# Weight tiles of a retention and feed-forward kernel: first parts rounded by a casting transfer on GpSimd's queue instead of by ScalarE

## The chip, the cores and the metric

One core of one Trainium2 chip. The metric is the device time of one execution in microseconds (us). The engines are called as the profile calls them: PE (TensorE, with PEld for its weight loads), DVE (VectorE), ACT (ScalarE), POOL (GpSimd) and SP (SyncE, which issues most transfers here).

## The reference, cut to what matters

Retention over 8 batches, 8 heads, 576 positions and 64 channels gives x of 4608 tokens by 512. A feed-forward with a rational function between two matrix products follows:

```python
ret = scores * Dmat[None, :, :, :]          # scores = q k^T / 8, Dmat = gamma ** (i - j), causal
x = matmul(ret, v)                          # reshaped to 4608 x 512
h = x @ w_in                                # 512 -> 2048
P = a[0] + a[1] * h + a[2] * h2 + a[3] * h3
Q = 1.0 + np.abs(b[0]) * np.abs(h) + np.abs(b[1]) * h2
return (P / (Q + 1e-06)) @ w_out            # 2048 -> 512
```

The weights come as float64. Products are made with operands in two parts: a first part, rounded to the type that PE reads fast (fp32r), and a second part, the rest. Each product is three matmuls: first by first, first by second, second by first.

## The kernel before

The 4608 tokens are nine blocks b of 512. The 2048 inner columns are sixteen tiles f of 128. One step of the main loop (L728) is one pair (b, f). `gemm1` (L478) makes h(b, f) in PSUM with twelve matmuls. `ffn_p` to `ffn_q3` (L489 to L535) make the rational function on ACT and DVE. `ffn_hi` (L549, ACT) and `ffn_lo` (L555, DVE or POOL by the table LO) make g, the two parts of its result. `gemm2` (L568) adds g times the second weights into the accumulators, three or four steps later (`lag`, L645). Steps 0 to 7 are block 0 with tiles 0 to 7, steps 8 to 23 block 1 with all sixteen, steps 24 to 31 block 0 with tiles 8 to 15; the other blocks follow. `half` is 8. Retention is done in slices before the loop and as "visits" inside it.

Weights: 32 tiles, w0_f of w_in and w1_f of w_out. `load_weight` (L165) brings the float64 bits of one, `split_weight` (L170), a generator, makes its two parts. It goes on by one yield whenever `split_step` (L663) is called, so its pieces lie in one to three steps:

- ACT writes c from the high words and scales the low words in place (L188, L189).
- DVE joins them in c (L192): this is the weight in float32.
- ACT copies c, rounded, into the first part (L199).
- DVE or POOL, by the table WLO (L71), subtracts it from c and so makes the second part (L201).

c comes from the pool `cnv` (L108), which has four buffers: ACT may write a fifth c only when the subtraction that reads the first is done. Four of the tiles (w1_0 to w1_3, called late) lie in other buffers and are left as they are.

Names: the profile leaves out numbers, so "c", "w", "g" and "p" stand for all tiles of that kind. With numbers, w1_10 is tile 10 of w_out, c1_10 its float32 form, g1_9 the result of block 1, tile 9, h1_12 its input to the function.

The order of the work on each engine is that of the program (`InOrder`, L78), and the program's order in a step is one of the lists of names at L33 to L57, the same in both versions. POOL has one queue of instructions: one that waits holds all behind it. In the part of the program that matters here (steps 8 to 21), u lies in PSUM (`free_at`) in most steps.

Of the kernel before, what the change touches and what calls it, by code (L numbers as in the profile page):

```python
# [13 lines left out]
F32R = mybir.dt.float32r  # L14
# [3 lines left out]
AF = mybir.ActivationFunctionType  # L18
# [3 lines left out]
P = 128  # L22
B, H, S, D = 8, 8, 576, 64
NT = B * S
DM = H * D
# [45 lines left out]
WLO = "vector pool pool pool pool pool pool vector vector pool vector vector vector vector pool pool vector vector pool vector pool vector pool vector pool vector pool pool pool pool vector pool".split()  # L71
# [18 lines left out]
def retention_ffn(ctx: ExitStack, tc: tile.TileContext, qkv, w_in, w_out, consts, masks, out):  # L90
# [13 lines left out]
    wts = ctx.enter_context(tc.tile_pool(name="wts", bufs=1))  # L104
# [12 lines left out]
    pe, act, dve, pool = (InOrder(tc, e) for e in (nc.tensor, nc.scalar, nc.vector, nc.gpsimd))  # L117
# [43 lines left out]
    parts = {}  # L161
    plain, held = {}, []
    step = -1
# [6 lines left out]
    def split_weight(k):  # L170


        nm = f"{k[0]}_{k[1]}"
        words = bits[k].bitcast(I32).rearrange("p (c w) -> p c w", w=2)
        low, high = words[:, :, 0], words[:, :, 1]
        late = k[0] == 1 and str(k[1]) in PLAIN
        if late:
            i = PLAIN.index(str(k[1]))
            if i < 2:
                held.append(op.tile([P, 2, DM], F32, tag=f"o{1 - i}", name=f"held{i}"))  # L180
            cf = plain[k[1]] = held[i % 2][:, i // 2, :]
            c = cf.bitcast(I32)
        else:
            c = cnv.tile([P, DM], I32, tag="c", name=f"c{nm}")
            cf = c.bitcast(F32)


        act.activation(cf, high.bitcast(F32), AF.Prelu, scale=math.ldexp(1.0, -112), alpha=-math.ldexp(1.0, 32))  # L188
        act.activation(low, low.bitcast(U32), AF.Copy, scale=math.ldexp(7.49, -32))  # L189
        yield  # L190
        yield
        dve.scalar_tensor_tensor(c, c, 3, low, ALU.logical_shift_left, ALU.bitwise_or)  # L192
        yield
        yield
        while late and step < PLAIN_TO + PLAIN.index(str(k[1])):
            yield
        w = wts.tile([P, 2, DM], F32R, tag=f"w{nm}", name=f"w{nm}")
        del bits[k]
        act.activation(w[:, 0, :], cf, AF.Copy)  # L199
        engine = dve if WLO[len(parts)] == "vector" else pool  # L200
        engine.tensor_tensor(w[:, 1, :], cf, w[:, 0, :].bitcast(F32), ALU.subtract)  # L201
        parts[k] = w

# [435 lines left out]
    half = NF // 2  # L639
# [18 lines left out]
    def split_start(n):  # L658
        for k in [k for _, k in zip(range(n), splits)]:
            going.append([split_weight(k), 0])  # L660
            next(going[-1][0])
# [66 lines left out]
    for i in range(len(steps) + lag(len(steps))):  # L728
        step = i
# [69 lines left out]
```

## Time and profile before

| | |
|---|---|
| median of 3 runs | 870.05 us (868.37 to 870.51) |
| profiled execution, its own time | 871.07 us |
| its span, first to last instruction | 869.0 us |
| PE busy | 849.4 us (98%) |
| DVE busy | 773.4 us (89%) |
| ACT busy | 665.6 us (77%) |
| POOL busy | 130.8 us (15%), 107 instructions |

The span is what the trace shows; the 2.07 us between it and the execution's own time lie around it. A share of busy time is an average over the whole span, and the part of the program in which the weights of the later steps are split is only some 115 us of it, so the views below are cut to windows of that part.

### The profile page before, as it was taken

The numbers are of one execution on the slowest core, as the hardware profiler recorded it, in microseconds if no ns is written. First come the engines' busy times: TensorE is split into PE (matmuls) and PEld (weight loads), VectorE is DVE, ScalarE is ACT, GpSimd is POOL, SyncE is SP. The second block draws the span as 40 slices with busy tenths as digits, with TensorE's granted clock in tenths as the row PEclk, the third lists the DMA queues.
The fourth block names the chain that finished last, engine by engine and source line by source line (L and its number), as shares of the span: only waits on it lengthen the run. The fifth ranks groups of instructions, "written<-read, shape, count | busy, mean of one in ns | idle before, by whom it ended". The sixth has DMA issues, their size and how long they took to land.

```text
span 869.0 us, 18739 instructions
## 1 busy us (share of the span) xinstructions
PE 849.4 (98%) x7574; PEld 727.2 (84%) x7574; DVE 773.4 (89%) x1221; ACT 665.6 (77%) x1240; POOL 130.8 (15%) x107
## 2 busy tenths in 40 slices
PE   8899999999999999999999999999999999999997
PEld 6666787778888888888888888888888888888886
DVE  4998999999899889888889888888898988888995
ACT  3888999988767778777877787777877787767775
POOL 2523333631001110111111100011111111000000
PEclk9999999999999999999999999999999999999999
DMA  9896000032121112111211121101211121001001
GB/s 341 320 340 232 1 2 0 1 99 101 48 98 50 49 50 98 49 50 50 97 50 50 50 89 60 47 30 37 87 47 50 49 98 50 1 2 48 1 1 48
DMA packets 20774, 64.55 MB, mean 74 GB/s; under 512 B 2512, under 2 KB 2640, under 8 KB 20688
## 3 DMA queue, kind: packets, MB, share of 16 engines
q1 hardware_dynamic: 20528, 63.10, 20.6%
q8 instruction: 59, 0.97, 0.4%
q14 instruction: 27, 0.22, 0.1%
q10 hardware_dynamic: 160, 0.26, 0.1%
HBM read 53.91 MB, written 9.44 MB: 73 GB/s over the span
## 4 chain that ended last, share of the span: by engine, by line
PE 83%; DVE 10%; ACT 4%; issue 1%; DMA 1%; SPq 0%; POOL 0%; ACTq 0%; DVEq 0%; POOLq 0%
PE acc L86 39%; PE h L86 36%; DVE p L86 4%; PE ps L86 4%; DVE v L86 3%; PE y L86 2%; DVE c L86 1%; ACT free_at L86 1%; PE psNone L86 1%; DMA qk<-in_qkv 1%; ACT bits L86 1%; ACT g L86 1%; ACT c L86 0%; DVE qk L86 0%; ACT p L86 0%
## 5 line engine op out<-in xcount | busy, mean ns | idle before, releaser
L86 PE MATMUL h<-xhi,w 128*128 128x512 f32 x1152 | 367.8, 381 | 3.8 <-DVE p L86 1.9
L86 PE MATMUL acc<-w,g 128*128 128x512 f32 x1584 | 366.9, 381 | 3.0 <-ACT o L86 1.6
L86 PEld LDWEIGHTS acc<-w,g 128*128 128x128 f32 x1584 | 296.5, 189 | 47.6 <-ACT o L86 2.0
L86 PEld LDWEIGHTS h<-xhi,w 128*128 128x128 f32 x1152 | 217.7, 189 | 37.9 <-DVE p L86 3.1
L86 ACT ACTIVATE p<-h,const_sb 128x512 f32<-128x512 f32 x144 | 111.6, 775 | 165.0 <-PE h L86 158.4
L86 PE MATMUL h<-xlo,w 128*128 128x512 f32 x576 | 218.4, 379 | 0.1
L86 DVE TENSOR_TENSOR p<-p,h 128x512 f32<-128x512 f32 x144 | 98.6, 684 | 42.5 <-ACT u L86 40.1
L86 PEld LDWEIGHTS h<-xlo,w 128*128 128x128 f32 x576 | 108.9, 189 | 16.7 <-issue 1.1
L86 DVE SCALAR_TENSOR_TENSOR p<-p,const_sb,h 128x512 f32<-128x512 f32 x144 | 107.3, 745 | 4.0
L86 ACT ACTIVATE v<-u,absb 128x512 f32<-128x512 f32 x129 | 103.2, 800 | 0.4 <-DVE p L86 0.2
L86 DVE TENSOR_TENSOR v<-v,u 128x512 f32<-128x512 f32 x131 | 101.4, 774 | 0.2 <-ACT v L86 0.2
L86 DVE SCALAR_TENSOR_TENSOR p<-v,p 128x512 f32<-128x512 f32 x140 | 98.6, 704 | 3.3
L86 DVE SCALAR_TENSOR_TENSOR p<-p,const_sb,u 128x512 f32<-128x512 f32 x131 | 99.2, 758 | 1.2 <-ACT u L86 1.2
L86 POOL TENSOR_TENSOR S<-S,const_sb 128x256 f32<-128x256 f32 x32 | 27.2, 850 | 453.4 <-DVE S L86 453.4
L86 DVE SCALAR_TENSOR_TENSOR v<-v,u 128x512 f32<-128x512 f32 x131 | 89.4, 683 | 0.0
L86 ACT ACTIVATE u<-u 128x512 f32<-128x512 f32 x131 | 82.6, 630 | 4.3
L86 ACT ACTIVATE g<-p 128x512 fp32r<-128x512 f32 x132 | 82.8, 627 | 3.5 <-DVE p L86 3.0
L86 ACT ACTIVATE u<-v 128x512 f32<-128x512 f32 x131 | 81.9, 625 | 0.8 <-DVE v L86 0.8
L86 DVE TENSOR_TENSOR g<-p,g 128x512 fp32r<-128x512 f32 x115 | 78.6, 683 | 0.7 <-ACT g L86 0.7
L86 ACT ACTIVATE u<-h 128x512 f32<-128x512 f32 x131 | 76.7, 585 | 2.5 <-DVE v L86 2.4
L86 ACT ACTIVATE kv<-kv,const_sb 128x64 f32<-128x64 f32 x232 | 58.2, 333 | 4.5 <-DMA kv<-in_qkv 4.5
L86 POOL TENSOR_TENSOR qk<-qk,const_sb 128x512 f32<-128x512 f32 x31 | 48.6, 1566 | 38.8 <-DMA qk<-in_qkv 38.7
(93 smaller groups left out, 713.7 us busy)
## 6 DMA issues: line engine op xcount, KB each, us to landing
qk<-in_qkv SPq DMA_DIRECT2D x36, 512.0 KB, 4.1
kv<-in_qkv SPq DMA_DIRECT2D x32, 512.0 KB, 5.5
bits<-in_w_in SPq DMA_DIRECT2D x16, 512.0 KB, 8.1
bits<-in_w_out SPq DMA_DIRECT2D x16, 512.0 KB, 7.3
out<-o SPq DMA_DIRECT2D x28, 256.0 KB, 3.7
kv<-in_qkv SPq DMA_DIRECT2D x4, 256.0 KB, 7.0
out<-o SPq DMA_DIRECT2D x8, 128.0 KB, 2.1
out<-last SPq DMA_DIRECT2D x2, 256.0 KB, 2.4
```

Of the source, the lines that this page charges most:

```text
L86: return lambda *a, **k: self.tc.keep_in_program_order(method(*a, **k))
```

## The change

For a tile whose third piece falls in step 8 or later, and which is not late, the copy on ACT is taken out. A transfer from c into the first part, which casts to fp32r, is issued on POOL's queue one yield earlier, and the subtraction is always POOL's.

```diff
         dve.scalar_tensor_tensor(c, c, 3, low, ALU.logical_shift_left, ALU.bitwise_or)
         yield
+        moved = step >= half and not late
+        if moved:
+            w = wts.tile([P, 2, DM], F32R, tag=f"w{nm}", name=f"w{nm}")
+            pool.dma_start(w[:, 0, :], cf)
         yield
         while late and step < PLAIN_TO + PLAIN.index(str(k[1])):
             yield
-        w = wts.tile([P, 2, DM], F32R, tag=f"w{nm}", name=f"w{nm}")
+        if not moved:
+            w = wts.tile([P, 2, DM], F32R, tag=f"w{nm}", name=f"w{nm}")
+            act.activation(w[:, 0, :], cf, AF.Copy)
         del bits[k]
-        act.activation(w[:, 0, :], cf, AF.Copy)
-        engine = dve if WLO[len(parts)] == "vector" else pool
+        engine = dve if WLO[len(parts)] == "vector" and not moved else pool
         engine.tensor_tensor(w[:, 1, :], cf, w[:, 0, :].bitcast(F32), ALU.subtract)
```

It holds for 17 tiles: w0_8 to w0_15 and w1_7 to w1_15. ACT has 17 instructions fewer, DVE 7 fewer, POOL 17 transfers and 7 subtractions more. Three places of the order show it.

DVE, at the end of the step in which c0_10 is joined; w0_9 is the second part of a weight tile, p and v are the rational function's.

```order
 L86 TENSOR_TENSOR v1_4_1258<-v1_4_1258,free_at_1045 128x512
 L86 SCALAR_TENSOR_TENSOR p1_3_1203<-v1_3_1202,p1_3_1203 128x512
-L86 TENSOR_TENSOR w0_9_1288<-c0_9_1185,w0_9_1288 128x512
 L86 SCALAR_TENSOR_TENSOR c0_10_1241<-c0_10_1241,bits0_10_907 128x512
 L86 TENSOR_TENSOR p1_5_1309<-p1_5_1309,h1_5_1294 128x512
```

The subtraction is gone from DVE, and what stood behind it moves up by one place. It is the same for w0_8, w0_11, w0_12, w0_13, w0_14 and w1_14.

ACT, around the writing of c1_12, which takes the buffer of c1_10.

```order
 L86 ACTIVATE free_at_1045<-v1_10_1554 128x512
 L86 ACTIVATE free_at_1045<-free_at_1045 128x512
-L86 ACTIVATE w1_10_1631<-c1_10_1535 128x512
-L86 ACTIVATE w0_14_1634<-c0_14_1538 128x512
 L86 ACTIVATE c1_12_1637<-bits1_12_1181 128x512
 L86 ACTIVATE bits1_12_1181<-bits1_12_1181 128x512
```

Two copies are gone in front of c1_12.

POOL, from g1_9 to g1_11, before:

```order
L86 TENSOR_TENSOR g1_9_1608<-p1_9_1505,g1_9_1608 128x512
L86 TENSOR_TENSOR w1_10_1631<-c1_10_1535,w1_10_1631 128x512
L86 TENSOR_TENSOR g1_10_1660<-p1_10_1555,g1_10_1660 128x512
L86 TENSOR_TENSOR w1_11_1683<-c1_11_1582,w1_11_1683 128x512
L86 TENSOR_TENSOR w0_15_1686<-c0_15_1585,w0_15_1686 128x512
L86 TENSOR_TENSOR g1_11_1723<-p1_11_1604,g1_11_1723 128x512
```

and with the change:

```order
L86 TENSOR_TENSOR g1_9_1608<-p1_9_1505,g1_9_1608 128x512
L86 DMA w1_10_1627<-c1_10_1535 128x512
L86 DMA w0_14_1629<-c0_14_1538 128x512
L86 TENSOR_TENSOR w1_10_1627<-c1_10_1535,w1_10_1627 128x512
L86 TENSOR_TENSOR w0_14_1629<-c0_14_1538,w0_14_1629 128x512
L86 TENSOR_TENSOR g1_10_1660<-p1_10_1555,g1_10_1660 128x512
L86 DMA w1_11_1679<-c1_11_1582 128x512
L86 DMA w0_15_1681<-c0_15_1585 128x512
L86 TENSOR_TENSOR w1_11_1679<-c1_11_1582,w1_11_1679 128x512
L86 TENSOR_TENSOR w0_15_1681<-c0_15_1585,w0_15_1681 128x512
L86 DMA w1_12_1729<-c1_12_1637 128x512
L86 TENSOR_TENSOR g1_11_1723<-p1_11_1604,g1_11_1723 128x512
```

Each subtraction now stands behind the transfer that writes its operand, on the same queue, and g1_11 stands behind three transfers and two subtractions that follow g1_10, where before two subtractions stood.

## Rows read from the trace of the kernel before

**Rows 1.** Busy time in windows: window, then us (count) by engine, PEclk, DMA share, GB/s.

```profile
103.72:132.31 28.59, 28.59 (x132) 24.86 (x132) 27.76 (x43) 27.55 (x44) 6.82 (x5) 1.00 0.01 1
132.31:157.13 24.82, 21.68 (x97) 17.87 (x97) 24.60 (x39) 23.08 (x39) 8.11 (x6) 1.00 0.00 0
157.13:191.10 33.97, 32.74 (x410) 27.43 (x410) 33.80 (x47) 29.09 (x59) 19.17 (x14) 1.00 0.11 33
300.00:700.00 400.00, 400.00 (x3850) 348.90 (x3849) 357.65 (x574) 302.97 (x591) 41.79 (x32) 1.00 0.17 57
```

**Rows 2.** Waits of PE, 75 to 195 us: us in total, times, longest us.

```profile
PE h L86 <- DVE p L86: 1.9, 3, 0.7
PE acc L86 <- ACT o L86: 1.6, 1, 1.6
PE h L86 <- ACT w L86: 1.3, 1, 1.3
PE y L86 <- issue: 0.5, 1, 0.5
PE acc L86 <- DVE w L86: 0.4, 1, 0.4
PE acc L86 <- POOL g L86: 0.3, 1, 0.3
```

**Rows 3.** Groups of instructions, 75 to 195 us: the pieces that split the weights.

```profile
L86 POOL TENSOR_TENSOR w<-c,w 128x512 fp32r<-128x512 f32 x10 | 13.5, 1353 | 22.9 <-ACT w L86 22.9
L86 ACT ACTIVATE w<-c 128x512 fp32r<-128x512 f32 x18 | 10.8, 623 | 0.0
L86 DVE TENSOR_TENSOR w<-c,w 128x512 fp32r<-128x512 f32 x8 | 5.4, 680 | 0.0
```

**Rows 4.** Timeline of DVE: start us, us; the subtraction of w0_8 and the next.

```profile
106.19 0.68 DVE L86 TENSOR_TENSOR w<-c,w 128x512 fp32r<-128x512 f32 x1
106.80 0.82 DVE L86 SCALAR_TENSOR_TENSOR c<-c,bits 128x512 int32<-128x512 int32 x1
```

**Rows 5.** DMA issues of the page: count, KB each, median us to landing.

```profile
bits<-in_w_in SPq DMA_DIRECT2D x16, 512.0 KB, 8.1
out<-o SPq DMA_DIRECT2D x28, 256.0 KB, 3.7
...
out<-o SPq DMA_DIRECT2D x8, 128.0 KB, 2.1
out<-last SPq DMA_DIRECT2D x2, 256.0 KB, 2.4
```

**Rows 6.** Timeline of POOL: the subtractions of g1_1, g1_9, g1_10 and g1_11.

```profile
101.76 1.27 POOL L86 TENSOR_TENSOR g<-p,g 128x512 fp32r<-128x512 f32 x1 [2.27 <-ACT g L86]
...
149.12 1.28 POOL L86 TENSOR_TENSOR g<-p,g 128x512 fp32r<-128x512 f32 x1 [4.68 <-ACT g L86]
...
155.56 1.27 POOL L86 TENSOR_TENSOR g<-p,g 128x512 fp32r<-128x512 f32 x1 [3.52 <-issue]
...
161.48 1.29 POOL L86 TENSOR_TENSOR g<-p,g 128x512 fp32r<-128x512 f32 x1 [1.80 <-issue]
```

**Rows 7.** Timeline of ACT: first part of g1_9; copies of w1_10, w0_14; c1_12.

```profile
148.37 0.68 ACT L86 ACTIVATE g<-p 128x512 fp32r<-128x512 f32 x1
...
150.06 1.14 ACT L86 ACTIVATE w<-c 128x512 fp32r<-128x512 f32 x2
152.08 0.88 ACT L86 ACTIVATE c<-bits 128x512 f32<-128x512 f32 x1 [0.88 <-POOL w L86]
```

**Rows 8.** Timeline of PE: the products of g1_10 and g1_11, 24 matmuls.

```profile
159.80 5.45 PE L86 MATMUL acc<-w,g 128*128 128x512 f32 x24
```

**Rows 9.** Timelines of DVE and POOL near 183 us: one operation alone, and one beside POOL.

```profile
182.92 1.77 DVE L86 SCALAR_TENSOR_TENSOR p<-p,const_sb,u 128x512 f32<-128x512 f32 x1
...
188.57 0.75 DVE L86 SCALAR_TENSOR_TENSOR p<-p,const_sb,u 128x512 f32<-128x512 f32 x1
...
182.67 1.48 POOL L86 TENSOR_TENSOR w<-c,w 128x512 fp32r<-128x512 f32 x1 [6.66 <-ACT w L86]
```

## The prediction

> **What bounds the kernel now.** I read the windows first, because the page's shares are averages over stages that differ. From 300 to 700 us PE is busy all the time and DVE and ACT have room (357.65 and 302.97 of 400) [rows 1]: what is gained or lost ahead of that stretch is carried to the end one to one, since nothing behind can catch up on PE. The change lies in 103 to 191 us. There DVE is busy 27.76 of 28.59, then 24.60 of 24.82, then 33.80 of 33.97 us, and ACT 23 to 29 us of each [rows 1], so DVE sets the pace with ACT close behind. POOL is busy 6.82, 8.11 and 19.17 us there and looks idle. The second view is PE's waits: from 75 to 195 us PE waited 6.0 us (1.9 + 1.6 + 1.3 + 0.5 + 0.4 + 0.3) [rows 2]. That sum is the ceiling of any gain in this part. The 1.6 us are for the accumulators' eviction on ACT where block 0 gives way to block 1, which stands in the program ahead of the first subtraction that DVE loses, so I leave it as it is: some 4.4 us can be had.
>
> **What the change removes.** ACT loses 17 copies of 623 ns; the window of [rows 3] counts 18, one of them of a tile that is not moved. DVE loses seven subtractions; its row counts 8, again with one that stays [rows 3]. On DVE the next instruction starts 0.61 us after such a subtraction starts (106.19 to 106.80) [rows 4], so the gain is 7 x 0.61 = 4.3 us if DVE alone sets the pace. ACT gains more in sum but waits for DVE in each step, so DVE's figure counts.
>
> **What it adds.** POOL gets seven subtractions more, at 1.35 us each (the mean of those it does now) [rows 3], and 17 transfers. POOL's queue is in order: each subtraction waits until its transfer has landed, and behind it wait the subtractions of g, which PE needs. So the price of a transfer is its whole time from issue to landing, D, during which POOL does nothing. No transfer of the trace is issued by POOL, goes from SBUF to SBUF or casts. The nearest rows are SP's: from 2.1 us for 128 KB to 8.1 us for 512 KB under the load of the first 80 us; between them lie 2.4 and 3.7 us for 256 KB, the size here [rows 5]. The DMA engines stand at a share of 0.00 to 0.11 here [rows 1], so the 8.1 is far. I take the two rows of the same size and a value a little above their middle, since POOL must make the descriptors by program: **D = 3.2 us**, with 2.1 and 8.1 kept as ends. How long POOL is held by the issue alone, before a second transfer may start, no row shows; it lies between nothing and D, and I take 1.0.
>
> The Trainium skill ("DMA: Bandwidth & Descriptors", section on the anatomy of one DMA on the gpsimd path) fits such a transfer as 2.0 us plus the bytes at 436 GB/s; for 256 KB that is an estimate of 2.6 us, and with it the sum below would come out 0.5 us faster than before instead of 0.7 us slower. No run here shows it yet.
>
> **Is POOL fast enough?** From the end of g1_1 at 103.0 [rows 6] to the start of g1_9 the new order has, in series, seven landings (w0_8, w0_9, w0_10, w0_11, w1_8, the pair w0_12 and w1_9, w0_13), eight subtractions of w, five of g at 1.28 and one issue of 1.0: 7D + 10.8 + 6.4 + 1.0 = 7D + 18.2. Before, g1_9's first part was there at 149.05 (148.37 + 0.68) [rows 7]; with five of DVE's subtractions gone by then it can be there 3.0 us earlier, at 146.1. So 103.0 + 7D + 18.2 must not exceed 146.1: D up to 3.6 is hidden, and with 3.2 POOL is there in time.
>
> **First place where it isn't hidden: c1_12.** ACT writes c1_12 into the buffer of c1_10, so it waits for the subtraction of w1_10. Already before, ACT waited 0.88 us for this and started at 152.08 [rows 7]. Now ACT could be there at 152.08 - 0.88 - 1.14 (two copies gone [rows 7]) - 3.0 = 147.1. But the transfer of w1_10 stands behind g1_9 on POOL: 146.1 + 1.28 (g1_9) + 3.2 + 1.35 = 152.0. ACT starts c1_12 at 152.0, 0.1 us earlier than before: the gain of five steps is turned into a wait of 4.9 us. PE doesn't see all of it at once, but the function of block 1, tile 12 stands behind c1_12 on ACT. After it two more copies are gone, so the lead is at most 1.3 us.
>
> **Second place: g1_11.** w0_14 is subtracted until 153.3, g1_10 follows its ACT part at 155.5 to 156.7 (before: 155.56 [rows 6]), then two issues, landings at 159.9 and 160.9, two subtractions to 162.6, the issue for w1_12 to 163.6, and g1_11 to 164.9. Before it ended at 162.77 [rows 6]. PE runs the 24 matmuls of g1_10 and g1_11 in 5.45 us from 159.80 on [rows 8], 0.227 each, and reads g1_11's second part at the fifteenth, at 159.80 + 14 x 0.227 = 163.0: before just in time, now 1.9 us late. Behind it PE waited 0.5 + 0.4 + 0.3 = 1.2 us for others [rows 2]; that absorbs 1.2. Sum: **+1.9 - 1.2 = +0.7 us**. From 103 to 150 us I put down nothing: PE's waits on DVE (1.9 us) go, and come back at c1_12.
>
> The profiled execution took 871.07 us, 1.02 above the median of 870.05. The changed execution would take 871.07 + 0.7 = 871.77, and as a median 871.77 - 1.02 = 870.75: I forecast **870.8 us**.
>
> **Rivals.** (1) *The relief arrives.* If the transfer takes 2.1 us and its issue next to nothing, c1_12 starts at 150.9 and g1_11 ends near 161.8, 1 us ahead of before; if then DVE's 4.3 us are mostly kept, the kernel gains 2.6 to 4.3 us: 865.7 to 867.4. For it: DVE is full [rows 1]. Against it: even then two thirds of the lead is eaten at c1_12. Chance 0.17.
> (2) *POOL becomes the bound* (slower). Above D = 3.6 each 0.1 us costs 0.7 us at g1_9 and 0.9 at g1_11. With D = 3.7, as the stores of this size take [rows 5], the end is 7 x 0.1 + 2 x 0.5 = 1.7 us later than in the sum, +2.4 (872.5); with 4.2 it is 7 x 0.6 + 2 x 1.0 = 6.2 later, +6.9 (877.0); with 8.1 it would be over 40. It decides from D = 3.75. For it: a cast and the making of descriptors are on no row. Against: landings in SBUF with idle DMA engines. Chance 0.3.
> (3) *DVE and POOL hinder one another.* One p of DVE took 1.77 us where the same took 0.75 alone; it began 0.25 us after POOL's subtraction of w1_15 [rows 9]. If each of the seven moved subtractions costs DVE such a 1.0 us, DVE loses 7.0 and gains 4.3: +2.7 us on top of the sum, 873.5. Against it: from step 10 to 20 u lies in PSUM, and DVE shows no such stretch beside POOL's work then. Chance 0.1.
> The Trainium skill ("SBUF — State Buffer", section Who interferes with whom) has the rule for it: a DVE instruction with two SBUF inputs contends with a GpSimd instruction that reads SBUF, and the later one is blocked. The pair at 183 us agrees, 1.77 against 0.75 [rows 9].
> That the change does nothing is excluded: the order shows the 17 transfers and the missing instructions.
>
> **How the numbers follow.** About 0.3%, 2.6 us, is what a measurement tells from no change. No change beyond that: 0.43 (forecast, D from 2.4 to 3.75). Faster: rival 1, 0.17. Slower: rivals 2 and 3, 0.40. The forecast's own range is 867.4 to 872.7. The range given reaches down into rival 1, to 866.2, and up through rival 2 at D = 4.3, 878; below lie some 7 in 100, above some 13.
>
> **What would show it.** Right: POOL's transfers land 3 to 3.5 us after issue; ACT waits 3 us or more for POOL w in front of one c near 148 to 152 us; PE waits for POOL g near 162 us; DVE's waits between 103 and 150 us stay small. Wrong towards faster: PE's waits for DVE p vanish and no wait for POOL takes their place. Wrong towards slower: D of 4 us or more, ACT waiting for POOL w several times from 120 us on, POOL's queue without a gap.

## The result, and the profile after

| | before | after |
|---|---|---|
| median | 869.34 us (868.37 to 870.51, 4 runs) | 877.80 us (877.44 to 878.57, 4 runs) |
| ratio | | 1.0098, 95% interval 1.0080 to 1.0115 |
| profiled execution, its span | 871.07, 869.0 us | 877.44, 875.7 us |
| DVE, ACT, POOL busy | 773.4, 665.6, 130.8 us | 779.6, 658.2, 147.4 us |

The change made the kernel 8.5 us slower. ACT lost work as it should, POOL gained it, and DVE, from which seven subtractions were taken, was busy 6 us longer.

The executions differ in their loading phase: the first product of g with a weight tile started at 78.6 us before and at 75.1 after, in a program that is the same up to there (75.1 to 79.9 in all profiles below). So I compare lengths: from the first start of such a product to the last, 785.3 us before (78.6 to 863.9) and 795.3 after (75.1 to 870.4).

PE's waits in the trace of after, 75 to 205 us (us in total, times, longest); they answer to [rows 2], to whose window the ten more microseconds add nothing for before:

```profile
PE h L86 <- DVE p L86: 5.4, 5, 2.5
PE acc L86 <- ACT o L86: 2.5, 1, 2.5
PE acc L86 <- POOL g L86: 1.5, 1, 1.5
PE acc L86 <- DMA w<-c: 1.3, 1, 1.3
PE y L86 <- issue: 1.1, 1, 1.1
PE ps L86 <- DVE kv L86: 1.0, 1, 1.0
PE acc L86 <- POOL w L86: 1.0, 1, 1.0
```

That is 13.8 us against 6.0, or 7.8 more. PE's timeline (start, us, instruction, wait before it) shows the eviction's, the longest, the one for g1_11 and two for w1_14 (its first part, then its second):

```profile
101.08 2.86 PE L86 MATMUL acc<-w,g 128*128 128x512 f32 x12 [2.54 <-ACT o L86]
...
157.28 0.48 PE L86 MATMUL h<-xhi,w 128*128 128x512 f32 x1 [2.52 <-DVE p L86]
166.31 2.43 PE L86 MATMUL acc<-w,g 128*128 128x512 f32 x10 [1.47 <-POOL g L86]
...
188.90 0.45 PE L86 MATMUL acc<-w,g 128*128 128x512 f32 x1 [1.29 <-DMA w<-c]
190.31 2.64 PE L86 MATMUL acc<-w,g 128*128 128x512 f32 x11 [0.96 <-POOL w L86]
```

The windows around 157 us (window, length, then busy by engine, PEclk, DMA share, GB/s) show the clock:

```profile
150.00:157.00 7.00, 4.75 (x23) 3.81 (x21) 6.91 (x8) 4.14 (x7) 3.89 (x4) 1.00 0.23 75
157.00:163.00 6.00, 5.72 (x19) 4.74 (x20) 5.89 (x10) 4.50 (x8) 3.23 (x4) 0.72 0.29 90
163.00:170.00 7.00, 5.53 (x26) 4.54 (x25) 6.97 (x4) 2.81 (x5) 6.98 (x8) 1.00 0.12 37
```

Behind the 2.52 us PE's granted clock is 0.72 on average over 6 us: for part of them TensorE ran at 1.2 GHz and not at 2.4, which costs (1 - 0.72) x 6.0 = 1.7 us. In before it is 1.00 throughout this part [rows 1]. Waits and clock give 7.8 + 1.7 = 9.5 us; the length grew by 10.0.

Why is DVE late? Its timeline (start, us), beside the subtraction of w0_8 and at the worst place:

```profile
102.84 1.69 DVE L86 SCALAR_TENSOR_TENSOR p<-v,p 128x512 f32<-128x512 f32 x1
...
164.00 1.00 DVE L86 SCALAR_TENSOR_TENSOR p<-v,p 128x512 f32<-128x512 f32 x1
164.92 6.57 DVE L86 TENSOR_TENSOR v<-v,u 128x512 f32<-128x512 f32 x1
```

POOL's timeline at the same places, with what it waited for:

```profile
100.33 0.57 POOL L86 DMA_DIRECT2D w<-c  x1
102.69 1.27 POOL L86 TENSOR_TENSOR w<-c,w 128x512 fp32r<-128x512 f32 x1 [1.79 <-DMA w<-c]
...
161.38 3.06 POOL L86 TENSOR_TENSOR w<-c,w 128x512 fp32r<-128x512 f32 x2 [2.77 <-DMA w<-c]
164.40 0.57 POOL L86 DMA_DIRECT2D w<-c  x1
164.99 1.27 POOL L86 TENSOR_TENSOR g<-p,g 128x512 fp32r<-128x512 f32 x1
166.21 1.28 POOL L86 TENSOR_TENSOR qk<-qk,const_sb 128x512 f32<-128x512 f32 x1
167.45 1.04 POOL L86 TENSOR_TENSOR kv<-kv,const_sb 128x512 f32<-128x512 f32 x1
168.45 1.26 POOL L86 TENSOR_TENSOR w<-c,w 128x512 fp32r<-128x512 f32 x1
169.68 1.26 POOL L86 TENSOR_TENSOR g<-p,g 128x512 fp32r<-128x512 f32 x1
```

POOL's subtraction starts when its transfer lands (the second of a pair when the first is done), 0.1 to 0.4 us before DVE's p<-v,p, which in this step is the one instruction besides c<-c,bits that has both inputs in SBUF. DVE's instruction then ends 0.57 us after POOL's (104.53 and 103.96). Eight of these p<-v,p, from 91.59 to 151.74 us, took 1.43 to 1.69 us where 0.68 is usual, some 7 us more in sum. The v<-v,u at 164.92 took 6.57 us beside five instructions of POOL and ended 0.55 us after the last (171.49 and 170.94): below this is called the block. In before DVE and POOL took turns at this place (DVE's timeline, then POOL's):

```profile
163.51 1.06 DVE L86 SCALAR_TENSOR_TENSOR p<-v,p 128x512 f32<-128x512 f32 x1
164.49 1.53 DVE L86 TENSOR_TENSOR v<-v,u 128x512 f32<-128x512 f32 x1
165.94 1.92 DVE L86 SCALAR_TENSOR_TENSOR c<-c,bits 128x512 int32<-128x512 int32 x1
...
163.98 1.49 POOL L86 TENSOR_TENSOR kv<-kv,const_sb 128x512 f32<-128x512 f32 x1
165.43 1.72 POOL L86 TENSOR_TENSOR w<-c,w 128x512 fp32r<-128x512 f32 x1
167.11 1.91 POOL L86 TENSOR_TENSOR g<-p,g 128x512 fp32r<-128x512 f32 x1
```

The transfers themselves (page, DMA issues: KB each, median us to landing) were quicker than I had taken:

```profile
w<-c POOLq DMA_DIRECT2D x17, 256.0 KB, 2.3
```

The timeline of ACT has the wait of c1_12 and, behind it, ACT's part p<-h for DVE's next p<-p,h; DVE's timeline shows what it did until then:

```profile
152.83 0.89 ACT L86 ACTIVATE c<-bits 128x512 f32<-128x512 f32 x1 [3.86 <-POOL w L86]
...
154.40 0.76 ACT L86 ACTIVATE p<-h,const_sb 128x512 f32<-128x512 f32 x1
...
153.27 2.42 DVE L86 SCALAR_TENSOR_TENSOR c<-c,bits 128x512 int32<-128x512 int32 x2
155.75 0.69 DVE L86 TENSOR_TENSOR p<-p,h 128x512 f32<-128x512 f32 x1
```

### The profile page after: what moved, and what is told of

The parts are those of the page before. It is cut to its first block, busy times and chain, and to the rows that moved or that the text cites. A ratio compares the mean times of both kernels' runs of the same rounds, so it can differ in the third digit from the quotient of the medians.

```text
span 875.7 us, 18789 instructions
## 1 busy us (share of the span) xinstructions
PE 848.6 (97%) x7574; PEld 726.4 (83%) x7574; DVE 779.6 (89%) x1214; ACT 658.2 (75%) x1223; POOL 147.4 (17%) x131
## 4 chain that ended last, share of the span: by engine, by line
PE 83%; DVE 10%; issue 3%; DMA 2%; POOL 1%; ACT 1%; SPq 0%; DVEq 0%; POOLq 0%; ACTq 0%
PE acc L86 38%; PE h L86 36%; DVE p L86 5%; PE ps L86 4%; DVE v L86 3%; PE y L86 2%; PE psNone L86 1%; DMA w<-c 1%; DVE c L86 1%; DMA qk<-in_qkv 1%; POOL w L86 1%; DVE qk L86 0%; POOL g L86 0%; PE ps_None L86 0%; DVE kv L86 0%
## 5 line engine op out<-in xcount | busy, mean ns | idle before, releaser
L86 DVE SCALAR_TENSOR_TENSOR p<-v,p 128x512 f32<-128x512 f32 x140 | 105.6, 754 | 3.3
L86 DVE TENSOR_TENSOR v<-v,u 128x512 f32<-128x512 f32 x131 | 106.6, 813 | 0.2 <-ACT v L86 0.2
L86 POOL TENSOR_TENSOR S<-S,const_sb 128x256 f32<-128x256 f32 x32 | 29.0, 907 | 450.8 <-DVE S L86 386.5
L86 DVE TENSOR_TENSOR g<-p,g 128x512 fp32r<-128x512 f32 x115 | 78.6, 684 | 0.7 <-ACT g L86 0.7
```

The costliest lines, as they stand in the source:

```text
L86: return lambda *a, **k: self.tc.keep_in_program_order(method(*a, **k))
```

## The experiments

Lengths, PE's waits from 75 to 205 us and the clock's loss come from one profiled execution each. The loss of the clock is the sum of (1 - PEclk) x 3 us over slices of 3 us below 0.995. The last column is DVE's longest instruction from 75 to 195 us.

| run | us, median | ratio to before, 95% interval | length, less 785.3 | waits, less 6.0 | clock | longest DVE instruction |
|---|---|---|---|---|---|---|
| after | 877.80 | 1.0098 [1.0080, 1.0115] | +10.0 | +7.8 | 1.7 | 6.57 |
| earlier issue | 876.72 | 1.0077 [1.0052, 1.0103] | +4.9 | +3.1 | 1.7 | 6.48 |
| shorter run | 876.39 | 1.0076 [1.0054, 1.0098] | +5.8 | +4.0 | 1.7 | 1.96 |
| longer run | 878.07 | 1.0103 [1.0071, 1.0134] | +8.4 | +5.9 | 1.7 | 4.12 |
| second parts only | 870.58 | 1.0015 [0.9997, 1.0033] | +0.7 | +0.2 | 0 | 1.95 |
| earlier and shorter | 872.69 | 1.0047 [1.0034, 1.0060] | +4.5 | +4.7 | 0 | 5.32 |
| first parts only | 876.88 | 1.0095 [1.0072, 1.0117] | +6.6 | +3.4 | 3.4 | 5.02 |
| all subtractions DVE's | 876.27 | 1.0094 [1.0079, 1.0109] | +7.1 | +3.3 | 3.4 | 3.07 |
| nine early tiles, earlier issue | 868.53 | 1.0002 [0.9988, 1.0017] | -0.8 | -0.6 | 0 | 1.96 |
| nine early tiles | 870.96 | 1.0031 [1.0019, 1.0043] | +2.4 | +1.9 | 0 | 1.94 |
| eight late tiles | 876.44 | 1.0094 [1.0080, 1.0107] | +7.0 | +4.1 | 3.4 | 6.58 |
| nine, earlier, shorter | 868.48 | 1.0004 [0.9991, 1.0017] | -0.3 | -0.7 | 0 | 1.76 |
| no issue ahead of the run | 875.18 | 1.0085 [1.0058, 1.0112] | +6.9 | +4.5 | 1.7 | 1.77 |

In every row waits and clock add up to the length to within 1.0 us: the loss is PE's, and these two hold it. Each ratio is to executions of before that were taken along with that run. A length and the medians can differ: +10.0 and +8.5 us for after, +4.9 and +7.2 for the earlier issue, the widest. So lengths are used to find where time went, ratios for what a version is worth.

**Earlier issue.** The transfer stands directly behind DVE's joining of c.

```diff
         dve.scalar_tensor_tensor(c, c, 3, low, ALU.logical_shift_left, ALU.bitwise_or)
-        yield
         moved = step >= half and not late
...
             pool.dma_start(w[:, 0, :], cf)
         yield
+        yield
```

> Same instructions as the change, but each transfer is issued right behind DVE's joining of c, one yield earlier, so in most steps ahead of the subtraction of g on POOL instead of behind it. Theory A (DVE and POOL hinder one another: a DVE instruction with both inputs in SBUF waits while POOL subtracts): POOL's subtraction of w now runs while DVE works on operands in PSUM, so the p<-v,p that took 1.43 to 1.69 us eight times in the changed kernel is back at 0.68 to 0.8 us at least six times out of eight, and the time falls by 5 us or more, to 866 to 873 us. Theory B (POOL's queue: waiting for landings delays g and c): POOL waits less for each landing (it idled 1.3 to 2.8 us per transfer), the wait of ACT for POOL at c1_12 (3.9 us) shrinks, the p<-v,p are as long as before or hit elsewhere, and the time falls by 1 to 3 us, to 875 to 877 us.

DVE's timeline of this run:

```profile
101.69 0.68 DVE L86 SCALAR_TENSOR_TENSOR p<-v,p 128x512 f32<-128x512 f32 x1
...
107.01 0.68 DVE L86 SCALAR_TENSOR_TENSOR p<-v,p 128x512 f32<-128x512 f32 x1
...
169.35 6.48 DVE L86 SCALAR_TENSOR_TENSOR p<-p,const_sb,u 128x512 f32<-128x512 f32 x1
```

Up to 130 us no p<-v,p is stretched: the landing no longer falls on it, and PE waits for no p of DVE until 150 us. So the stretches are POOL's subtraction beside DVE, as theory A has it. Its time missed (866 to 873 us expected, 876.72 measured): the block came back elsewhere, beside kv, w, g, w, qk, and the clock fell behind waits near 180 us. By its ratio this run can't be told from after.

**Shorter run.** Unit 8's scaling of q goes from POOL to DVE, that of v to ACT, so two instructions leave the run beside which DVE stood still.

```diff
-SCALES = "scalar pool pool vector pool vector pool scalar pool".split()
-SCALES_Q = "vector vector vector pool pool vector vector pool pool".split()
+SCALES = "scalar pool pool vector pool vector pool scalar scalar".split()
+SCALES_Q = "vector vector vector pool pool vector vector pool vector".split()
```

> The change, with the scaling of unit 8's q given to DVE and that of its v to ACT, so that POOL has two instructions fewer between g1_11 and g1_12, where DVE's v<-v,u took 6.57 us. Theory A, with the addition that DVE does not get its turn as long as POOL has the next instruction ready: the long v<-v,u falls to 3 us or less, and the time by 3 to 5 us, to 873 to 875 us. Theory B: the length of that DVE instruction does not come from POOL; it stays above 6 us, g1_12 comes 2.5 us earlier, and the time falls by 0 to 1.5 us, to 876.5 to 878 us.

v<-v,u took 1.90 us instead of 6.57, and POOL had a gap of 0.48 us behind g. The eight p<-v,p stayed, and so did PE's wait near 157 us (2.57 us) and the fall of its clock. The time missed theory A's 873 to 875 us and can't be told from after's either.

**Longer run.** The opposite: v of unit 8 is scaled on POOL twice over, by two instructions instead of one.

```diff
-            engine.tensor_tensor(v, v, gv_sb[:, 0:H].unsqueeze(2).broadcast_to([P, H, D]), ALU.mult)
+            for _ in range(2 if n == 8 else 1):
+                engine.tensor_tensor(v, v, gv_sb[:, 0:H].unsqueeze(2).broadcast_to([P, H, D]), ALU.mult)
```

> The change, with the scaling of unit 8's v done twice on POOL (so that unit's part of the output is scaled once too often): one POOL instruction of about 1.25 us more between g1_11 and g1_12. Theory A with the addition: the long v<-v,u of DVE grows from 6.57 to 7.5 to 8.0 us, and the time by 1 to 1.5 us, to 878.5 to 879.5 us. Theory B: the DVE instruction keeps its 6.57 us within 0.2, g1_12 is 1.25 us later, and the time grows by 0 to 1.3 us.

Missed: 4.12 us and not 7.5 to 8. DVE ended in the middle of the second kv, which reads what the first wrote. So the number of instructions alone doesn't set how long DVE stands.

**Second parts only.** ACT copies as before, no transfer; the subtractions of the moved tiles are all POOL's.

```diff
-            w = wts.tile([P, 2, DM], F32R, tag=f"w{nm}", name=f"w{nm}")
-            pool.dma_start(w[:, 0, :], cf)
+            pass
...
-        if not moved:
+        if True:
```

> The second half of the change alone: the first parts are again copied by ACT and no transfer is made, all moved second parts are subtracted by POOL. Theory A: POOL's subtractions start where ACT's copies end instead of where transfers land; they meet p<-v,p two or three times instead of eight and no DVE instruction takes over 2.2 us; DVE keeps 1 to 3 us of its 4.3: 866 to 869 us. Theory B: without landings POOL is never the last, all of DVE's relief arrives: 865 to 867 us, and every p<-v,p before 155 us is at 0.8 us or less.

Within 0.3% of before. Seven subtractions fewer on DVE gave nothing that can be seen, and without the transfers most of the 8.5 us is gone.

**Earlier and shorter.** Both edits above together.

> The transfer is issued one yield earlier, and unit 8's two scalings are taken from POOL, so both kinds of stretch that the trace of after shows on DVE should go: the eight p<-v,p of 1.4 to 1.7 us and the block beside a gapless run of POOL. Everything is told from the first to the last product of g with w (before 785.3 us, after 795.3, with only the earlier issue 790.2, with only the shorter run 791.1). Theory A (DVE and POOL hinder one another, and a late DVE makes PE wait): no DVE instruction over 2.5 us, at most four p<-v,p over 0.75; PE's waits from 75 to 205 us are 6 to 8 us (before 6.0), TensorE's clock stays at 1.00 there, the length is 785 to 788 us, the time 869 to 872. Theory B (POOL's queue: what waits for a landing holds g and c): the queue is the same but for two instructions, so 875 to 878. A third, that the two repairs are worth their sum: 795.3 - 5.1 - 4.2 = 786.0 us.

Between the theories: 872.69, by its ratio better than either repair alone (the intervals overlap a little), but a block of 5.32 us came back, beside w, g, w, qk, right behind the issue of another transfer.

**First parts only.** The transfers stay, the subtractions go where the table WLO has them.

```diff
-        engine = dve if WLO[len(parts)] == "vector" and not moved else pool
+        engine = dve if WLO[len(parts)] == "vector" else pool
```

> The transfers stay; the seven subtractions that were moved from DVE to POOL go back to DVE (the table WLO alone decides). Theory A: DVE loses the relief of 7 x 0.61 = 4.3 us, and at least four of the eight p<-v,p of after (those beside w0_8, w0_9, w0_11, w0_13) are back at 0.68, which gives some 4 x 0.9 = 3.6 us: the two nearly cancel, and the block beside the gapless run of POOL at some 165 us (g, qk, kv, w1_12, g) stays. Time 875 to 879. Theory B: seven subtractions of 1.29 us and their waits for a landing leave POOL's queue, so g and c come as in before: 869 to 873, and POOL's waits for landings fall from 21.7 us to under 13.

Theory A's time held, theory B's did not: POOL waited 14.1 us for landings instead of 21.7, and nothing was won. The four stretches named are gone; a p<-v,p of 5.02 us stands beside g, qk, kv and w. Near 157 us, in DVE's and PE's timelines:

```profile
154.97 0.69 DVE L86 TENSOR_TENSOR p<-p,h 128x512 f32<-128x512 f32 x1 [0.42 <-ACT free_at L86]
...
156.50 0.48 PE L86 MATMUL h<-xhi,w 128*128 128x512 f32 x1 [2.47 <-DVE p L86]
```

Here DVE was not the last: it waited for ACT, which had waited 3.85 us at c1_12, and PE's wait is as long as in after.

**All subtractions DVE's.**

```diff
-        engine = dve if WLO[len(parts)] == "vector" and not moved else pool
+        engine = dve if WLO[len(parts)] == "vector" or moved else pool
```

> The transfers stay; all seventeen subtractions are DVE's, so POOL issues transfers and reads no weights at all. This takes away both what theory A blames (POOL's subtraction beside p<-v,p) and what theory B blames (POOL waiting for a landing), and leaves theory C: the transfers' own reads and writes of SBUF hinder DVE. DVE has 10 x 0.61 = 6.1 us more to do than in before. A and B: p<-v,p at 0.68 beside every transfer in flight (but those beside a g of POOL), POOL waits for no landing, c is not held; DVE's work makes it some 3 to 8 us slower than before, 873 to 878. C: p<-v,p or its neighbours still stretched beside transfers with POOL idle, and over 878.

No p<-v,p up to 160.23 us is stretched. Most of them start just after a landing, but the one at 160.23 took 0.69 us with two transfers in flight (issued from 157.86 on; DVE waited for them until 161.50), and DVE's other instructions between an issue and its landing took their usual time: theory C falls, as far as these show. The Trainium skill ("SBUF — State Buffer", section Who interferes with whom) gives DMA ports of its own, apart from the engines'; this run agrees, with that 0.69 us. DVE had more to do, waited 2.3 us for landings, and PE's clock fell twice, behind waits of 2.0 and 2.8 us. The second of them, in DVE's and PE's timelines:

```profile
156.10 0.69 DVE L86 TENSOR_TENSOR p<-p,h 128x512 f32<-128x512 f32 x1 [0.90 <-ACT free_at L86]
...
157.62 0.48 PE L86 MATMUL h<-xhi,w 128*128 128x512 f32 x1 [2.79 <-DVE p L86]
```

Nothing of DVE is stretched here, yet ACT waited 4.20 us at c1_12 (for a subtraction of DVE), DVE 0.90 us for ACT, and PE longer than in after. So a late c1_12 is enough for this wait and the fall behind it.

**Nine early tiles with the earlier issue.** Only tiles up to w0_13 are moved.

```diff
-        moved = step >= half and not late
+        moved = half <= step < 18 and not late
```

> The earlier issue, and only for the nine tiles up to w0_13 (steps below 18); the eight tiles behind it are as in before. A version that might beat both kernels: up to 130 us the earlier issue showed no stretched p<-v,p with seven subtractions fewer on DVE, and its stretches came after. Theory A: length from the first to the last product of g with w 783 to 786 us (before 785.3): DVE is up to 5 x 0.61 = 3.1 us ahead when the late steps come, of PE's waits 3.9 us in the trace of before after 130 us are DVE's or ACT's; no block over 2.5 us. Time 867 to 870, with a gain of at most 2 us. Theory B: nine waits for landings remain on POOL: 870 to 874.

No difference from before. The first two waits of PE for p, 0.70 and 0.45 us in before, shrank to one of 0.27; all waits together fell by 0.6 us in the profile, which the measurement can't tell from nothing.

**Nine early tiles, eight late tiles.** The two halves of the change, each alone, issued where the change issues them (steps below 19, and from 19 on).

```diff
-        moved = step >= half and not late
+        moved = half <= step < 19 and not late
```

```diff
-        moved = step >= half and not late
+        moved = step >= 19 and not late
```

> Only the nine tiles up to w0_13 are moved, and issued where the change issues them; the eight tiles behind them are as in before. This keeps the p<-v,p that the landings stretch (six of after's eight lie here besides the first) and takes away the late part, with its block of some 6 us. Theory A1 (the single stretches carry the loss): 7 x 0.9 = 6.3 us less 5 x 0.61 = 3.1 us leave DVE some 3 us late at 145 us, PE stalls and its clock falls: 873 to 876, more than half of the 8.5 us. Theory A2 (the late part carries it: POOL lets go of a stock of ready instructions at once, behind a wait for a landing, and DVE stands still beside it): 869 to 872, no DVE instruction over 2.5 us, clock 1.00 from 130 us on.

> The other half alone: only the eight tiles from w1_10 on are moved; the nine before them are as in before. Theory A1: two or three stretched p<-v,p, and the block is worth what the shorter run gave, 1 to 2 us: 870 to 872. Theory A2: a gapless run of POOL of four or more instructions, beside it a DVE instruction of 4 to 7 us, at some 160 to 175 us; PE's waits 10 to 12 us from 75 to 205 us, with a fall of its clock worth 1.7 us: 873 to 877. If the halves are independent, this run's gain or loss and that of the other add up to the 8.5 us of the change.

The median of before taken along with both is 867.87. The halves cost 870.96 - 867.87 = 3.1 and 876.44 - 867.87 = 8.6 us; they aren't independent, since together they cost 8.5. The nine with the earlier issue cost nothing that can be seen (1.0002 against 1.0031, the intervals apart): so the stretches beside the landings are what the early half costs. Theory A2 held in both: the late part by itself is enough, with the 6.58 us block and, as not expected, two falls of the clock.

**Nine, earlier, shorter.** A try for a faster version.

> The nine early tiles with the earlier issue, and unit 8's two scalings taken from POOL (q to DVE, v to ACT): a try for a version that beats both. With the nine and the earlier issue alone the late part still showed p<-v,p 1.10, v<-v,u 1.53 and c<-c,bits 1.96 in a row beside POOL, as before does. If DVE's lost time there is paid by PE, two instructions fewer on POOL give 1 to 2 us: 866.5 to 868. If PE's waits come from elsewhere (o of ACT, the first p), no difference: 868 to 870.

The same as before. No version here is faster than before by anything that can be measured.

**No issue ahead of the run.** What made DVE stand through five instructions of POOL, where in before it took turns with the same five? Here w1_12 alone is not moved, so no transfer is issued ahead of them.

```diff
-        moved = step >= half and not late
+        moved = step >= half and not late and nm != "1_12"
```

> The change without one of its seventeen tiles, w1_12, whose first part stays ACT's copy. So POOL's run g, qk, kv, w, g keeps its five instructions, and only the issue of a transfer directly ahead of it is gone. In all runs so far a DVE instruction that stood still through three to five instructions of POOL had such an issue directly ahead of the run (after, the earlier issue, the longer run, first parts only, all subtractions on DVE, late eight); where the same five came without an issue ahead (before, the nine tiles), DVE and POOL took turns: 1.06 or 1.10, 1.53, 1.9 us. Theory X (it takes the issue ahead of the run): DVE and POOL take turns, no DVE instruction over 2.5 us from 155 to 175 us, POOL's kv, w and g stretched to 1.5 to 1.9. Theory Y (a run of four or five instructions is enough): a DVE instruction of at least 3.5 us beside g, qk and kv, before w1_12 and its copy have any part in it. The time tells little: the eight stretched p<-v,p stay, so X 874.5 to 877, Y 876 to 878.5.

POOL's timeline of this run:

```profile
164.62 1.27 POOL L86 TENSOR_TENSOR g<-p,g 128x512 fp32r<-128x512 f32 x1
165.85 1.73 POOL L86 TENSOR_TENSOR qk<-qk,const_sb 128x512 f32<-128x512 f32 x1
167.55 1.49 POOL L86 TENSOR_TENSOR kv<-kv,const_sb 128x512 f32<-128x512 f32 x1
169.00 1.97 POOL L86 TENSOR_TENSOR w<-c,w 128x512 fp32r<-128x512 f32 x1
170.93 1.26 POOL L86 TENSOR_TENSOR g<-p,g 128x512 fp32r<-128x512 f32 x1
```

DVE's beside it:

```profile
165.43 1.01 DVE L86 SCALAR_TENSOR_TENSOR p<-v,p 128x512 f32<-128x512 f32 x1
166.36 1.77 DVE L86 TENSOR_TENSOR v<-v,u 128x512 f32<-128x512 f32 x1
168.06 1.74 DVE L86 SCALAR_TENSOR_TENSOR c<-c,bits 128x512 int32<-128x512 int32 x1
```

The same five instructions without a gap, and now DVE gets its turn between them; POOL's are the longer ones. Theory X held. The length fell from 795.3 to 792.2; 1.0 us of that is PE's wait for g1_11, ahead of the block, which shrank from 1.47 to 0.49, so the block was worth some 2 of the 10 us. Why an issue ahead should matter is not settled: the edit also shifted the two engines against each other (v<-v,u began 0.07 us ahead of g in after, and 0.51 us into qk here).

## Why the prediction was right or wrong

The range held the time by luck: its upper end stood for transfers of 4.3 us, and they took 2.3. The forecast, no change and 870.8 us, was 7.0 us too low. Two mechanisms made the loss: the third rival's, to which I gave 0.1, and the forecast's own, POOL's queue behind the landings, which stood at the places named but cost PE more than I put down.

**What the change removes** was right in kind. The seven subtractions are gone, but their 4.3 us never reached PE: moving them alone gave 870.58 us, no gain.

**The price of a transfer** was mis-sized to the safe side: 2.3 us from issue to landing against the 3.2 taken, 0.57 us of POOL for an issue against 1.0. The estimate of 2.6 us by the fit in the Trainium skill ("DMA: Bandwidth & Descriptors", section on the anatomy of one DMA on the gpsimd path) was nearer than mine; the measured 2.3 decides. The second rival's condition, transfers of 3.75 us and more, is not met in the median, and first parts only, which took seven subtractions off POOL's queue, won nothing. Single landings still cost: see c1_12, g1_11 and w1_14 below.

**"From 103 to 150 us I put down nothing"** is the step that failed first. PE's waits for p of DVE up to 150 us did not go; they rose from 0.70 + 0.45 + 0.70 = 1.85 to 0.66 + 0.54 + 0.50 + 1.14 = 2.84 us, and the eviction's wait, which I left as it is though the transfer of w1_7 comes ahead of it (88.81 us), from 1.64 to 2.54 (2.54 to 2.57 in every run with a stretched p<-v,p near 91 us, 1.76 to 1.79 with the earlier issue). The 3.0 us by which g1_9 was to come earlier were a delay: its subtraction began 46.9 us behind the first product after the eviction (101.08 to 147.94) and in before 45.4 (103.72 to 149.12). The ground is my sentence against the third rival, that DVE shows no stretch from step 10 to 20 because u lies in PSUM. p<-v,p has two inputs in SBUF in every step. In before POOL's work hardly fell on it in these steps (from 95 to 153 us p<-v,p took 0.68 or 0.69 us, once 0.80); the landing put it there. The earlier issue took the landing away from it, and the stretches went.

**c1_12** is the second step that failed, by its cost. ACT did wait for POOL, 3.86 us against my 4.9, but in the sum PE sees nothing of it. PE's wait there was 2.52 us against 1.28 in before, and behind it came the fall of the clock, 1.7 us, which no term of mine had. DVE was the last before PE, by some 0.6 us: behind the stretched p<-v,p (1.61) and c<-c,bits (two in 2.42 us, before 1.56) its p<-p,h began at 155.75, while ACT had its part ready at 155.16. Where DVE was not held the wait is no shorter, though: it was 2.47 and 2.79 us in first parts only and with all subtractions DVE's, where DVE itself waited for ACT. In the five profiles in which ACT waited only 0.9 us at c1_12, before among them, PE waited 0.9 to 1.3 us and the clock did not fall there.

**g1_11.** Named rightly: PE waits 1.47 us for POOL's g; I had 1.9. The other half, that 1.2 us of waits behind it would absorb this, was wrong: they rose to 1.3 + 1.0 + 1.1 + 1.0 = 4.4 us. 1.1 + 1.0 of them, for y and kv, go with the block: without it (no issue ahead of the run) they are gone. The other 1.3 + 1.0 are for w1_14, for which I had no term: its transfer, issued at 183.06, was the slowest with 5.7 us, and POOL's subtraction stood behind it; in before PE waited 0.4 us for this tile. They stay without the block, 1.2 + 0.8 us.

So the ten microseconds of the profile are, from the front: 0.9 (eviction), 1.0 (p up to 150 us), 1.2 (p at 157), 1.7 (clock), 1.5 (g1_11) and 3.2 (behind it), 9.5 in all.

**The third rival** had a mechanism that is there, at the wrong instruction and the wrong tiles, and for a part of the loss. It counted a stretch for each subtraction moved away from DVE. But the eight stretches stand beside any subtraction of POOL that a landing starts, and the block beside g and unit 8's scalings too. Of the 9.5 us some 1.9 go with the stretches up to 150 us (the nine early tiles alone gave +1.9 of waits) and some 2 with the block; the rest stands at c1_12 with the clock, at g1_11 and at w1_14, where POOL's queue waits for landings. The Trainium skill's rule ("SBUF — State Buffer", section Who interferes with whom) agrees with each single stretch: the later instruction ended 0.54 to 0.57 us after the earlier.

## What to carry to other kernels

Before work is moved to GpSimd, or what starts it is changed, look which DVE instructions have both inputs in SBUF and lie where it will now run; idle time of GpSimd is not free while DVE is full. A transfer on GpSimd's queue sets by its landing when the next GpSimd instruction starts, so one yield earlier or later in the program can decide; and whatever waits for the buffer or the tile behind it, here c1_12 and w1_14, has to be followed to PE with a price of its own. And where PE's waits grow, look at the granted clock behind the longest: here it cost 1.7 us on top of a wait that grew by 1.2.

## What the runs showed of the hardware

- A DVE instruction with two SBUF inputs can take as long as several instructions of GpSimd beside it. With a transfer's issue directly ahead of the run it ended 0.55 to 0.57 us after the run's last, in six profiles: 6.57, 6.58, 6.48 (five instructions), 5.32, 5.02 (four), 3.07 us (three). Without one, in before and in four runs, the two engines took turns and no DVE instruction there took over 1.96 us. A gap of 0.48 us, and a second instruction that reads what the first wrote, also let DVE in behind an issue (one run each). The one edit that took the issue away ended the block; the cause inside the engine stays open.
- TensorE's granted clock fell to the lower level for part of some 6 us, at a cost of 1.7 us each time. It did so behind waits of 2.5 to 2.8 us at 157 to 159 us in six profiles, behind 2.84 us for g and 2.54 us of the eviction (first parts only), behind 2.0 us of the eviction (all subtractions DVE's), and near 180 us behind 2.2 us (eight late tiles) and behind 1.6 and 0.9 us in a row (earlier issue). It did not behind the eviction's wait of 2.5 to 2.6 us in after and four other profiles, nor behind 2.47 us at 156.50 (first parts only). The length of the wait alone does not tell.
- A casting transfer of 256 KB within SBUF, issued by GpSimd, took 2.2 us at least, 2.3 in the median and 5.7 at most, and its issue held GpSimd 0.53 to 0.72 us.
